# Replacing a build-time list scheduler by stored orders, engine choices and PSUM banks in a four-layer attention kernel

## The chip, the cores and the metric

One core of one Trainium2 chip runs the whole kernel. The metric is the device time of a launch in microseconds; most executions of one kernel agree within 0.3%. A ratio is the mean time of one kernel's fast runs over the mean of the other's from the same rounds on the same chip, so it is not quite the ratio of the medians beside it. 1% of the kernel before is 4.5 us.

PE is the matmul engine, PEld its weight loads, ACT the scalar engine, DVE the vector engine, POOL the general-purpose engine, SP the sync engine, from whose queue all DMAs here start.

## The reference

Four residual layers on x of 2048 rows by 512 features in bfloat16, 32 heads of 16 features; layers A and B alternate, and the second pair reuses the weights of the first:

```python
x = x + A(layernorm(x)); x = x + B(layernorm(x))
x = x + A(layernorm(x)); x = x + B(layernorm(x))
# A, linear attention:
phi = lambda t: where(t > 0, t + 1, exp(t)) + 1e-6
kv = einsum("bhsd,bhse->bhde", phi(k), v);  z = phi(k).sum(s)
o  = (phi(q) @ kv) / (phi(q) @ z + 1e-6)
# B, causal softmax attention over a window of 256 rows:
p = softmax(where(0 <= i - j < 256, q @ k.T * 0.25, -1e9));  o = p @ v
# both end with o.reshape(B, S, D) @ wo
```

A needs a sum over all rows before its first output, so it is a barrier. B's exponentials are most of ACT's work.

## The kernel before

The kernel is not written as loops. It records some 2740 operations in a graph, each with its engine (or two allowed engines), an estimated cost, a priority key, what it reads and writes, and its PSUM tiles. Then, while the program is built, a list scheduler plays the graph against its costs and decides three things: the order on each engine, the engine of each copy that ACT and DVE can both do, and the PSUM bank of each tile (1011 of them reuse one of eight banks).

```python
def pick_banks(banks, held, need):
    if "S" in need:                                   # scores: aligned pairs of banks
        pairs = [b for b in (0, 2, 4, 6) if b in banks and b + 1 in banks]
        n = need["S"] // 2
        return [x for b in pairs[:n] for x in (b, b + 1)] if len(pairs) >= n else None
    free = sorted(banks, key=lambda b: (held[b ^ 1] is None, held[b ^ 1] == "S", -b))
    ...
def schedule(g, par):
    ...
    while done < len(ops):
        t = heapq.heappop(events)                     # simulated time
        ...
        for e in engines:                             # free engine: the ready operation with the lowest key
            if free_at[e] > t: continue
            while ready[e]:
                k, i = heapq.heappop(ready[e])
                ...                                   # skip it if no bank is free
            o.eng, o.t0 = e, start
            got = pick_banks(banks, held, need) if need else []
            ...
            o.deps.extend(u for u in banks.pop(b)[1] if u not in o.deps)
```

The last line: a tile's first matmul waits for the last reader of the tile that had the bank before. A second pass (unchanged) turns all dependencies into semaphore waits; each engine's instruction stream is its list, in the order of the list.

The other piece touched is the transpose of a normalised tile, on PE with a copy out of PSUM, or by a DMA; and the first layer's use of it:

```python
    def transpose(self, name, src, out, rd, wr, key, by_pe):
        if not by_pe:
            return self.on("SP", name, lambda e: e.dma_start_transpose(out(), src()), key, (1310, ...), rd=rd, wr=wr)
        ps = Tile(1, K.cls)
        ...                                           # four 128x128 transposes, then a copy on ACT or DVE
    def layer_a_keys(self, ph, base):
        for t in range(T):
            self.norm(t, ..., [("XQ", t)], True)      # True: transposes of the first stage on PE
            self.a_k(t, k); self.a_v(t, k + 0.05); self.a_q(t, ...)
```

The softmax here doesn't subtract the row's maximum and nothing guards it: scores larger than these inputs give would overflow.

Of the kernel before, what the change touches and what calls it, by code (L numbers as in the profile page):

```python
# [8 lines left out]
ALU = mybir.AluOpType  # L9
# [13 lines left out]
    same=0.0, lat_t=4300, cap_s=8, cap_d=2, cap_e=6, mode=100, sem=35, ring_x=3, wait_s=200,  # L23
# [63 lines left out]
def pick_banks(banks, held, need):  # L87

    if "S" in need:
        pairs = [b for b in (0, 2, 4, 6) if b in banks and b + 1 in banks]  # L90
        n = need["S"] // 2
        return [x for b in pairs[:n] for x in (b, b + 1)] if len(pairs) >= n else None
    free = sorted(banks, key=lambda b: (held[b ^ 1] is None, held[b ^ 1] == "S", -b))
    n = sum(need.values())
    return free[:n] if len(free) >= n else None


def schedule(g, par):

    ops = g.ops  # L100
    for o in ops:
        o.outs, o.nout, o.rdy, o.t0 = [], len(o.deps), 0.0, None
        o.soft = []
        for t in o.tiles:
            t.banks, t.left = None, len(t.users)

    for o in ops:
        for t in o.tiles:
            if t.soft and t.users[0] is o:
                o.soft.extend({d for u in t.users[1:] for d in u.deps if d.i < o.i} - set(o.deps))  # L110
        o.nout += len(o.soft)
        for d in o.soft:
            d.outs.append(o)
    for o in ops:
        for d in o.deps:
            d.outs.append(o)
    engines = ("PE", "ACT", "DVE", "POOL", "SP")
    free_at = dict.fromkeys(engines, 0.0)
    ready = {e: [] for e in engines}
    last_mode = [None, None]  # L120
    banks = {b: (0.0, []) for b in range(8)}
    used = {"S": 0, "D": 0, "E": 0, "K": 0}
    held = [None] * 8
    cap = {"S": par["cap_s"], "D": par["cap_d"], "E": par["cap_e"], "K": 2}
    pending = []
    events = [0.0]
    done = 0

    def release(o):
        if o.nout == 0:  # L130
            heapq.heappush(pending, (o.rdy, o.i))
            heapq.heappush(events, o.rdy)

    for o in ops:
        release(o)
    order = []
    giving = []
    while done < len(ops):
        if not events:
            stuck = [o.name for o in ops if o.t0 is None][:12]  # L140
            raise RuntimeError(f"stuck {stuck} banks {used} {[ (e, [ops[i].name for _, i in ready[e]][:6]) for e in engines]}")
        t = heapq.heappop(events)
        while events and events[0] <= t + 0.5:
            t = max(t, heapq.heappop(events))
        while pending and pending[0][0] <= t:
            _, i = heapq.heappop(pending)
            for e in ops[i].engs:
                k = ops[i].key
                if e == "ACT" and len(ops[i].engs) > 1:
                    k += par["act_bias"]  # L150
                heapq.heappush(ready[e], (k, i))
        while giving and giving[0][0] <= t:
            _, b, cls, users = heapq.heappop(giving)
            banks[b] = (0.0, users)
            held[b] = None
            used[cls] -= 1
        for e in engines:
            if free_at[e] > t:
                continue
            back = []  # L160
            pick = None
            held_back = False
            if e == "PE" and par["same"]:
                ready[e] = [(ops[i].key + (par["same"] if ops[i].mode != last_mode[0] else 0.0), i) for _, i in ready[e]]
                heapq.heapify(ready[e])
            while ready[e]:
                k, i = heapq.heappop(ready[e])
                o = ops[i]
                if o.t0 is not None:
                    continue  # L170
                need = {}
                for x in o.tiles:
                    if x.banks is None:
                        need[x.cls] = need.get(x.cls, 0) + x.n
                if need:
                    if any(used[c] + m > cap[c] for c, m in need.items()) or pick_banks(banks, held, need) is None:
                        back.append((k, i))
                        if "S" in need:
                            n = sum(1 for x in giving if x[0] <= t + par["wait_s"])
                            held_back = held_back or len(banks) + n >= 4  # L180
                        continue
                if held_back and o.end is None and e == "PE" and any(x.banks is None for x in o.tiles):
                    back.append((k, i))
                    continue
                pick = o
                break
            for x in back:
                heapq.heappush(ready[e], x)
            if pick is None:
                continue  # L190
            o = pick
            occ, lat = o.engs[e]
            start = t
            if e == "PE":
                if last_mode[0] is not None and o.mode != last_mode[0]:
                    occ += par["mode"]
                    lat += par["mode"]
                last_mode[0] = o.mode
            o.eng, o.t0 = e, start
            o.end = start + occ  # L200
            o.fin = start + lat + par["sem"]
            need = {}
            for x in o.tiles:
                if x.banks is None:
                    need[x.cls] = need.get(x.cls, 0) + x.n
            got = pick_banks(banks, held, need) if need else []
            for x in o.tiles:
                if x.banks is None:
                    b = got.pop(0)
                    x.banks = [b]  # L210
                    held[b] = x.cls
                    used[x.cls] += x.n
                    o.deps.extend(u for u in banks.pop(b)[1] if u not in o.deps)
                x.left -= 1
                if x.left == 0:
                    for b in x.banks:
                        heapq.heappush(giving, (o.fin, b, x.cls, list(x.users)))
                    heapq.heappush(events, o.fin)
            free_at[e] = o.end
            heapq.heappush(events, o.end)  # L220
            order.append(o)
            done += 1
            for c in o.outs:
                lat_seen = o.end if (e == "PE" and set(c.engs) == {"PE"}) else o.fin
                if o not in c.soft:
                    c.rdy = max(c.rdy, lat_seen)
                c.nout -= 1
                release(c)
    order.sort(key=lambda o: (o.t0, o.i))
    return order  # L230
# [85 lines left out]
class Plan:  # L316
# [33 lines left out]
    def load(self, name, emit, nbytes, wr, key):  # L350
        us = nbytes / 0.2e6 * 1000
        return self.on("SP", name, emit, key, (us, us + 2000), wr=wr)

    def setup(self):
# [13 lines left out]
        for i, (n, f, b, r) in enumerate(seq):  # L368
            self.load(n, f, b, r, key + i)
        i = len(seq)  # L370
        self.load("wBv", lambda e: e.dma_start(K.wBv[:], K.B_wqkv.rearrange("(k p) c -> p k c", p=P)[:, :, 1024:1536]), 524288, [("wBv",)], key + i)
        self.load("wBo", lambda e: e.dma_start(K.wBo[:], K.B_wo.rearrange("(k p) c -> p k c", p=P)), 524288, [("wBo",)], key + i + 1)

        def pool(name, emit, key, ns, **kw):
            return self.on("POOL", name, emit, key, (ns, ns + 60), **kw)
# [43 lines left out]
    def norm(self, t, key, xn_slot, out, wr, by_pe):  # L419
# [4 lines left out]
        self.on("POOL", "eps", lambda e: e.tensor_scalar(K.ve[:, t, :], K.mv[:, t, 1:2], LN_EPS, None, op0=ALU.add), key + 0.02, (190, 260), rd=[("mv", t)], wr=[("ve", t)])  # L424
# [95 lines left out]
    def layer_a_keys(self, ph, base):  # L520
        self.cls = "E"
        for t in range(T):
            k = 100 * ph + t
            self.norm(t, k - 0.5, t % self.par["ring_x"], lambda t=t: self.XQ[:, :, t * P:(t + 1) * P], [("XQ", t)], True)
            self.a_k(t, k)
            self.a_v(t, k + 0.05)
            self.a_q(t, 200 + 4 * (t // 4) + 0.2 * (t % 4) - self.par["k_aq2"])
# [218 lines left out]
    def middle(self, ph):  # L746
# [19 lines left out]
        for i in range(2):  # L766
            self.on("POOL", "zero", lambda e, i=i: e.memset(flat(1536 * i, 1152), 0.0), base - 5, (600, 660), wr=self.room[i])
# [34 lines left out]
class Kernel(Plan):  # L802
# [16 lines left out]
    def run(self):  # L819
# [4 lines left out]
        with ExitStack() as cx:  # L824
# [37 lines left out]
            with nc.Block() as blk:  # L862
                @blk.tensor
                def _(e):
                    play("PE", e)
# [57 lines left out]
```

## Time and profile before

| | before |
|---|---|
| time, median | 453.22 us (453.1 to 453.32) |
| profiled span | 451.5 us |
| busy: PE, DVE, ACT | 89%, 82%, 81% |
| first exponential of the first B layer | 79.9 us |
| from there to that layer's last exponential | 170.4 us |
| from there to the first exponential of the second B layer | 42.1 us |
| from there to its last exponential | 150.7 us |
| tail | 8.4 us |

The five stretches are the stages 1 to 5. They are cut at exponentials because ACT's exponentials mark where each B layer begins and ends whatever the order. Idle time is worth reading only on the engine that leads a stage: PE in 1 and 3, ACT (with PE and DVE close) in 2, ACT in 4. The lines themselves stand in the prediction. Two cautions on the trace of the kernel before: its first exponential starts at 79.75 us, so the cut at 79.9 is 0.15 us late; and it records 7540 matmuls for 7620 weight loads, so 80 matmuls are missing and PE's idle time is read too high.

### The profile page before, as it was taken

How to read it: one execution, taken by the hardware profiler on the slowest of the kernel's cores; microseconds unless marked ns; L12 is line 12 of the kernel's file. 1: busy time of each engine (PE TensorE's matmuls, PEld its weight loads, DVE VectorE, ACT ScalarE, POOL GpSimd, SP SyncE). 2: the span in 40 equal slices, each digit the busy share in tenths (PEclk: the TensorE clock that was granted, in tenths of full speed). 3: DMA queues.
4: the chain of work that ended last, by engine and by line, in shares of the span. 5: the costliest groups of instructions: out<-in, count | busy, mean ns of one | idle time of the engine just before them, and what ended most of it. 6: DMA issues, size and time to landing. Idle time of an engine off the chain costs nothing.

```text
span 451.5 us, 17346 instructions
## 1 busy us (share of the span) xinstructions
PE 400.2 (89%) x7540; PEld 267.7 (59%) x7620; DVE 372.4 (82%) x835; ACT 364.6 (81%) x539; POOL 83.2 (18%) x177
## 2 busy tenths in 40 slices
PE   3899989998998988889999998999899999998765
PEld 1445667666565655556656776766566666665443
DVE  3997798899899989987887839799998999986543
ACT  1555625998999999899999443599999999999982
POOL 7869012012011201120110040210000011000000
PEclk9999999999999999999999999999999999999867
DMA  8800003424433533356422000163344643434321
GB/s 268 290 3 1 1 1 72 109 62 86 97 73 95 89 83 94 70 104 94 73 69 52 15 1 3 49 121 85 91 100 108 102 99 86 111 91 109 68 51 48
DMA packets 63307, 36.39 MB, mean 81 GB/s; under 512 B 43264, under 2 KB 58624, under 8 KB 63232
## 3 DMA queue, kind: packets, MB, share of 16 engines
q1 hardware_dynamic: 63232, 35.28, 34.1%
q8 instruction: 60, 0.98, 1.0%
q14 instruction: 15, 0.12, 0.1%
HBM read 6.29 MB, written 2.10 MB: 19 GB/s over the span
## 4 chain that ended last, share of the span: by engine, by line
ACT 38%; PE 31%; DVE 23%; POOL 4%; issue 3%; POOLq 0%; DVEq 0%
ACT pb L659 28%; PE ps L461 14%; PE ps L475 7%; ACT pb L693 6%; PE ps L718 4%; DVE stats L422 3%; PE ps L645 3%; DVE xres L588 3%; DVE xn L426 2%; DVE pk L486 2%; DVE XQ L486 2%; DVE tE L485 2%; POOL rs L425 2%; ACT pb L660 2%; DVE pb L700 2%
## 5 line engine op out<-in xcount | busy, mean ns | idle before, releaser
L659 ACT ACTIVATE pb<-ps 128x1024 bf16<-128x1024 f32 x224 | 213.3, 1051 | 6.7 <-PE ps L645 6.1
L718 PEld LDWEIGHTS ps<-vB,pb 128*128 128x128 bf16 x2880 | 80.1, 96 | 18.4 <-DVE vA L450 2.7
L718 PE MATMUL ps<-vB,pb 128*128 128x34 bf16 x2880 | 85.8, 178 | 3.4 <-ACT pb L659 0.8
L424 POOL TENSOR_SCALAR ve<-mv 128x1 f32<-128x1 f32 x64 | 17.3, 270 | 299.1 <-DVE mv L423 297.6
L475 PE MATMUL ps<-xT,wBp 128*128 128x128 bf16 x1024 | 67.2, 219 | 2.4 <-DVE o L730 0.7
L666 DVE TENSOR_TENSOR pb<-pb,tri 128x512 bf16<-128x512 bf16 x128 | 53.7, 419 | 18.4 <-ACT pb L659 12.3
L484 ACT ACTIVATE tE<-ps 128x512 bf16<-128x512 f32 x64 | 39.0, 612 | 36.5 <-PE ps L475 18.9
L475 PEld LDWEIGHTS ps<-xT,wBp 128*128 128x128 bf16 x1024 | 58.0, 98 | 11.2 <-issue 3.8
L461 PE MATMUL ps<-wA,XQ 128*128 128x512 bf16 x240 | 61.6, 387 | 2.2 <-DVE o L730 0.4
L645 PE MATMUL ps<-XQ,kB 32*128 32x256 bf16 (+3 forms) x1024 | 50.3, 271 | 13.8 <-ACT pb L659 6.1
L693 ACT ACTIVATE pb<-ps 128x512 bf16<-128x512 f32 x112 | 59.0, 628 | 2.4 <-PE ps L683 2.2
L588 DVE TENSOR_TENSOR xres<-ps,xres 128x512 bf16<-128x512 f32 x64 | 43.8, 685 | 10.1 <-PE ps L461 9.7
L422 DVE BATCH_NORM_STATS2 stats<-xres 128x6 f32<-128x512 bf16 x64 | 43.3, 681 | 4.0 <-DMA xres<-in_A_x_dram 3.6
L645 PEld LDWEIGHTS ps<-XQ,kB 32*128 32x128 bf16 x1024 | 15.3, 93 | 43.8 <-ACT pb L659 23.4
L700 DVE TENSOR_TENSOR pb<-pb,tri 128x1024 bf16<-128x1024 bf16 x56 | 37.4, 674 | 3.9 <-ACT pb L693 3.9
L425 POOL TENSOR_TENSOR rs<-ve,negh 128x1 f32<-128x1 f32 x64 | 38.0, 594 | 5.3
L461 PEld LDWEIGHTS ps<-wA,XQ 128*128 128x128 bf16 x256 | 21.9, 98 | 25.1 <-issue 2.3
L461 PE MATMUL ps<-wBo,oT 128*128 128x512 bf16 x106 | 30.8, 406 | 5.2 <-DVE xn L426 1.4
L475 PE MATMUL ps<-XQ,wA 128*128 128x128 bf16 x512 | 35.3, 219 | 0.1
L426 DVE TENSOR_SCALAR xn<-xres,mv,rs 128x512 bf16<-128x512 bf16 x64 | 28.6, 453 | 6.3 <-POOL rs L425 5.8
L475 PEld LDWEIGHTS ps<-XQ,wA 128*128 128x128 bf16 x512 | 30.2, 98 | 4.7 <-DVE XQ L486 0.6
L461 PE MATMUL ps<-wBv,xT 128*128 128x512 bf16 x110 | 29.6, 380 | 3.3 <-DVE o L730 1.0
(78 smaller groups left out, 463.1 us busy)
## 6 DMA issues: line engine op xcount, KB each, us to landing
vB<-vA SPq DMA_DIRECT2D x128, 68.0 KB, 2.1
kB<-vA SPq DMA_DIRECT2D x64, 128.0 KB, 2.1
out_dram<-xres SPq DMA_DIRECT2D x16, 128.0 KB, 2.0
wA<-in_A_wqkv_dram SPq DMA_DIRECT2D x3, 512.0 KB, 5.9
xres<-in_A_x_dram SPq DMA_DIRECT2D x2, 512.0 KB, 8.5
pb<-in_B_wqkv_dram SPq DMA_DIRECT2D x1, 1024.0 KB, 9.9
xres<-in_A_x_dram SPq DMA_DIRECT2D x3, 256.0 KB, 5.0
wAo<-in_A_wo_dram SPq DMA_DIRECT2D x1, 512.0 KB, 8.6
```

Source lines behind the costliest of these rows:

```text
L422: self.on("DVE", "stats", lambda e: e.bn_stats(K.stats[:, t, :], K.xres[:, t, :]), key, dve(512), rd=[("xres", t)], wr=[("stats", t)])
L425: self.on("POOL", "pow", lambda e: e.tensor_tensor(K.rs[:, t, :], K.ve[:, t, :], K.negh[:], ALU.pow), key + 0.03, (540, 590), rd=[("ve", t ...
L461: m = e.matmul(K.ps(ps), lhs(c), rhs(c), start=c == 0, stop=c == 3)
L475: m = e.matmul(K.ps(ps)[:, f * P:(f + 1) * P], w(c, f), xT(c), start=c == 0, stop=c == 3)
L484: self.on("ACT", "E", lambda e: e.activation(K.tE[:, s, :], K.ps(ps), ACT.Exp, bias=0.0), key, act(512), wr=[("tE", s)], ps=[ps])
L588: self.on("DVE", "res", lambda e: e.tensor_tensor(K.xres[:, t, :], K.ps(po), K.xres[:, t, :], ALU.add), key, dve(512), rd=[("xres", t)], w ...
L645: m = e.matmul(K.ps(ps[gq])[:, 256 * b:256 * b + ns[b]], K.kB[rows, j % 4, 2 * f + b, :, :], K.XQ[rows, f, q:q + ns[b]], start=True, stop= ...
L659: return e.activation(x, bank().rearrange("p g (b n) -> p g b n", b=2), ACT.Exp, bias=0.0, scale=0.25)
L666: return e.tensor_tensor(x, x, K.tri[:, 0, :].unsqueeze(1).unsqueeze(1).to_broadcast([P, 4, 2, 64]), ALU.mult)
L693: return e.activation(K.pb[:, sl, 2 * h:2 * h + 2, :, o:o + 64], i, ACT.Exp, bias=0.0, scale=0.25)
L700: return e.tensor_tensor(x, x, K.tri[:, 1, :].unsqueeze(1).to_broadcast([P, 16, 64]), ALU.mult)
L718: m = e.matmul(K.ps(ps)[:, 34 * u:34 * u + 34], K.pb[:, (b // 2) % 3, gq, f, o:o + P], K.vB[:, (b // 2) % 4, b % 2, r, :], start=i == 0, s ...
```

## The change

Its intent: search for a better schedule off line, starting from critical chains, and store what was found, in place of a scheduler that decides greedily. 338 lines of diff, cut to the core:

```diff
+def place(g):
+    ops = g.ops
+    raw = zlib.decompress(b85decode("".join(TABLE)))
+    n = len(ops)
+    order = [ops[raw[2 * k] + 256 * raw[2 * k + 1]] for k in range(n)]
...
+        o.eng = ("PE", "ACT", "DVE", "POOL", "SP")[raw[2 * n + o.i]]
...
+        x.banks = [raw[3 * n + k]]
...
+            before = held[x.banks[0]]
+            if before:
+                assert all(u.t0 < o.t0 for u in before.users)
+                o.deps.extend(u for u in before.users if u not in o.deps)
-def pick_banks(banks, held, need): ...
-def schedule(g, par): ...
-        order = schedule(self.g, self.par)
+        order = place(self.g)
...
-            self.norm(t, ..., [("XQ", t)], True)
+            self.norm(t, ..., [("XQ", t)], t < self.par["pe_first1"])      # pe_first1=5
-            self.load(n, f, b, r, key + i)
+            self.load(n, f, b, r, key + i if n[0] == "x" or n[:3] in ("wAk", "wAv", "wAq") else 104 + 0.01 * i)
+TABLE = ( ... 60 lines of text ... )
```

Besides the stored schedule: eleven of 16 first-stage transposes go by DMA, weights that are needed late are loaded late, and costs of POOL operations and loads are corrected (which matters only to the search).

## The prediction

> **What bounds the kernel now.** I read first the busy shares and the 40 slices, then a table of engine busy time cut at four moments that I took from the timeline (first exponential of the first sliding-window layer at 79.9 us, its last at 250.3, first of the second such layer at 292.4, last at 443.1), then the chain of waits, and the timeline of the start.
>
> ```profile
> PE 400.2 (89%) x7540; PEld 267.7 (59%) x7620; DVE 372.4 (82%) x835; ACT 364.6 (81%) x539; POOL 83.2 (18%) x177
> ```
>
> Three engines are above 80%: no single bound, and no removal on one engine alone can pay in full. By stage (columns: stretch, its length, busy us of PE, PE weight load, DVE, ACT, POOL, then clock, DMA share, GB/s):
>
> ```profile
> 0.00:79.90 79.90, 66.63 (x713) 41.96 (x725) 64.78 (x145) 38.48 (x67) 40.57 (x85) 1.00 0.30 90
> 79.90:250.30 170.40, 154.72 (x3143) 102.33 (x3169) 150.04 (x344) 161.24 (x236) 21.54 (x50) 1.00 0.41 83
> 250.30:292.40 42.10, 39.61 (x623) 30.30 (x631) 29.75 (x68) 17.08 (x30) 9.58 (x18) 1.00 0.05 14
> 292.40:443.10 150.70, 135.19 (x3046) 91.31 (x3072) 125.32 (x276) 147.17 (x206) 11.54 (x24) 0.97 0.42 94
> 443.10:451.50 8.40, 4.01 (x35) 1.76 (x36) 2.49 (x5) 0.60 (x1) 0.00 (x0) 0.67 0.10 33
> ```
>
> The reader is to see that the limits change. Stage 1 (first linear layer) and stage 3 (second one) are PE's: 39.6 of 42.1 us in stage 3. Stage 4 is ACT's, 147.2 of 150.7: only 3.5 us are idle there. Stage 2 is held by three engines at once; ACT leads with 161.2 of 170.4, so 9.2 us are idle. Stage 5 is a tail in which nobody works much.
>
> ```profile
> 4.09 1.81 POOL spread L378
> 8.02 1.02 POOL spread L394
> 9.37 0.83 POOL spread L394
> 12.50 0.72 DVE xn L426
> 13.55 0.87 DVE tE L485
> ...
> 326.04 7.60 ACT pb L659 x8
> 333.63 1.96 ACT pb L693 x4
> 335.61 7.60 ACT pb L659 x8
> ```
>
> These are the chain that ended last (start, us, what). At the start it runs through constants that POOL builds ahead of the first normalisation. In stage 4 it is a metronome of eight exponentials at 0.95 us and four at 0.49, 9.56 us per block of 128 rows: an order cannot shorten that. The first PE work:
>
> ```profile
> 7.75 1.24 PE L438 MATMUL ps<-ident,xn 128*128 128x128 bf16 x8 [7.75 <-DVE xn L426]
> 9.05 3.57 PE L461 MATMUL ps<-wA,XQ 128*128 128x512 bf16 x8
> 13.61 1.90 PE L461 MATMUL ps<-wA,XQ 128*128 128x512 bf16 x8
> ```
>
> PE starts at 7.75 us, and its first eight wide matmuls take 3.57 us where the next eight take 1.90.
>
> **What the Trainium skill says.** (1) Perfetto Trace Analysis, Identifying the Most-Contended Engine: matmul busy share is a poor measure of distance to the roofline, weight-load busy time a better one; and under Optimization Strategy, a kernel with several regimes may gain by interleaving them. The trace agrees: weight loads are busy 59% where matmuls show 89%, and the five stages have different leaders. (2) TensorE: Matmul & The Clock Gate, The HAM clock gate: matmuls of the first some 3.4 us run at half clock. The 3.57 against 1.90 us above agrees; starting earlier moves this loss, it doesn't remove it. (3) DMA: Bandwidth & Descriptors, DMA Transpose (X-bar): a plain DMA transpose is issued only from the sync or scalar engine. Here all 73 come from the sync queue, at a median 1.27 us of that queue and 2.5 us to landing. (4) TensorE again, Architectural detail: ACT and DVE are strict FIFO. So an instruction listed too early stops all behind it; what an order is worth is just these waits (waits on ACT in the first 80 us: 8.4 us for the query and 7.8 us for the key matmuls).
>
> **The change part by part.** No arithmetic changes; I counted both programs' orders.
>
> *Transposes.* Eleven of 16 tiles in stage 1 (from the sixth on) go by DMA. PE loses 44 matmuls of 128x128: twelve take 0.67 us in the chain, so a tile 0.22 us, 2.5 us together. Eleven copies out of PSUM go too: at 0.49 us of ACT or about 0.34 of DVE (estimate from their 597 and 412 ns less the overlap). Added: eleven sync-queue issues, 11 x 1.27 = 14 us, between about 12 and 50 us where that queue and the DMA are empty (2 to 5 GB/s in slices 3 to 6). They lie beside other work, if they come early enough; the order lists the first eight in a row, right behind the 1 MB weight load.
>
> *PE lists.* Ahead of the first score matmul: minus 2.5 us of transposes, plus 16 query matmuls of 0.056 us (64 take 3.57 us), 0.9: net minus 1.6 us. Between the last score of one layer and the first of the next: minus eight half-products of two wide matmuls each (four value, two output, two windowed-value projections) at 0.445 us (four take 0.89), 3.6 us; minus one group of 24 value matmuls, 0.6; plus two query halves, 0.9, and one denominator group, 0.39: net minus 2.9 us. That work isn't gone: it is listed inside the window layers beside ACT's work (there PE is busy 154.7 of 170.4 us, and 135.2 of 150.7).
>
> *Engine choice.* Copies that either engine can do: in stage 2 ACT has 30 other operations beside the exponentials in place of 35, 5 x 0.48 = 2.4 us less. In stage 4 it has four in place of six, 1 us less. DVE takes them at 0.60 each; over the whole kernel ACT loses 14 operations and DVE gains three.
>
> *Start.* The order puts the first epsilon operation behind seven small POOL constants (0.2+1.8+0.2+0.2+0.3+0.1+0.2 = 3.0 us) instead of eleven plus the big memset, which the trace shows ending at 5.9 us. From 0.8 us that is about 4.1 us, just when the first statistics are done (3.0 + 0.65 + 0.2). Then PE starts near 6 us, not 7.75: minus 1.8 us. Other weights load later; 4.5 MB now stand ahead of the first DMA transpose, at 308 GB/s 15 us, which five tiles of PE work (5 x about 2.8 us) just cover.
>
> *Banks and order.* This is the part without a count. What it can win is the idle time that waits leave. Stage 1: from 9.05 to 79.9 us PE has 60.6 us of listed work (by spacing, e.g. 0.23 us per wide matmul), so some 10 us are lost, 1.7 of it cold clock; I give the search 2 us. Stage 2: 9.2 us idle on ACT; I give it a quarter, 2.5 us. Stage 4: 3.5 idle; 0.7.
>
> *Sum.* Stage 1: 1.8 + 1.6 + 2.0 = 5.4, so 74.5 us. Stage 2: 2.4 + 2.5 = 4.9, so 165.5. Stage 3: 2.9, so 39.2. Stage 4: 1.0 + 0.7, so 149.0. Tail 8.4 unchanged: the chain last exponential, values, division, transpose, output projection, residual, store is the same. Together 436.6 us of span, 14.9 less; the time is 1.7 us above the span before, so 438.3 us, minus 3.3%.
>
> **The rivals.** (a) *The orders give little.* ACT's list in stages 2 and 4 still holds all 400 exponentials, and a list order on paper may be out of step with the chip: a strict FIFO then waits. For it: three engines are near full, so what one wait frees another takes. Against it: the lists are really shorter where the stage's leader is (ACT minus 2.4, PE minus 1.6 and 2.9). Only those 6.9 us plus 1 us in stage 4 would remain: 445 us. (b) *DVE becomes the bound of stage 2.* It takes five copies, 3.0 us, on top of 150.0 of 170.4 busy. At 165.5 us it would be 92% busy; this would halve the stage's gain: 441 us. (c) *DMA transposes come late.* Each lands 2.5 us after issue and they share the rings with 3.5 to 4.5 MB of loads. If the sixth tile came at 22 instead of 18 us, PE would idle some 4 us unless other tiles' work fills it: 441 to 442 us. (d) *The search worked better than I think*: all of ACT's idle time in stage 2 and 5 us of stage 1's go: 6.7 + 3 us more, 429 us.
>
> **Range and chances.** Centre 438.3. (b) and (c) give the upper side, both with part of (a) 446; (d) the lower, 430. The 2% line is 444.2: only (a), or (b) with (c), lies above. I give 0.86 to faster by over 2%, 0.13 to the same, 0.01 to slower, since nothing is added on an engine that leads.
>
> **What would show it right or wrong.** PE's first matmul near 6 us; first exponential near 74.5; ACT's idle time between first and last exponential of the first such layer down from 9 to about 6.5 us; 39 us between the layers with PE over 94% busy; the second such layer 149 us at 9.56 us a block; a tail of 8.4. It is wrong if PE shows long waits for the DMA-written XQ between 15 and 30 us, if ACT waits for scores as often as before, or if the granted clock, now 0.97 in stage 4, falls in more places, because PE then idles in longer pieces.

## The result, and the profile after

The changed kernel takes 434.0 us median (432.52 to 434.44, 4 runs), the kernel before 453.22: ratio 0.957, 95% interval 0.9546 to 0.9595. The forecast was 438.3, in a range of 430 to 446.

Busy shares of the kernel after, then its table by stage (columns as in the prediction):

```profile
PE 402.1 (93%) x7576; PEld 265.4 (61%) x7576; DVE 374.7 (87%) x838; ACT 355.3 (82%) x525; POOL 83.3 (19%) x177
```

```profile
0.00:73.46 73.46, 63.39 (x682) 41.20 (x683) 62.42 (x140) 32.72 (x59) 39.91 (x83) 1.00 0.44 117
73.46:239.39 165.93, 160.79 (x3219) 102.51 (x3218) 154.19 (x353) 160.03 (x231) 22.22 (x52) 1.00 0.42 85
239.39:276.75 37.36, 37.09 (x600) 29.41 (x599) 30.17 (x67) 16.52 (x31) 9.51 (x18) 1.00 0.06 20
276.75:425.22 148.47, 137.28 (x3025) 90.37 (x3024) 124.53 (x273) 145.99 (x204) 11.69 (x25) 0.97 0.41 95
425.22:432.70 7.48, 3.52 (x61) 1.95 (x58) 3.41 (x8) 0.00 (x0) 0.00 (x0) 0.92 0.12 38
```

The arithmetic is the same (PE busy 402.1 us against 400.2 with 80 matmuls unrecorded, DVE 374.7 against 372.4; ACT 355.3 against 364.6, since it has 14 copies fewer); about half of what went is time in which a stage's leader waited. Read the leader of each stage. In stage 2 ACT idled 170.4 - 161.2 = 9.2 us and now 165.9 - 160.0 = 5.9; PE idles 5.1 us there where it idled 15.7 by its trace and 10.7 in e6. In stage 3 PE idled 2.5 us (2.1 in e6, with every matmul recorded) and now 0.3: it is busy 99%. In stage 4 ACT's idle time went from 3.5 to 2.5 us. Stage 3 of e6:

```profile
250.01:292.16 42.15, 40.06 (x630) 30.32 (x631) 29.80 (x68) 17.08 (x31) 9.58 (x18) 1.00 0.05 15
```

Stage 1 needs a second cut, at 15 us, before and after:

```profile
0.00:15.00 15.00, 6.73 (x31) 3.02 (x32) 7.70 (x18) 3.67 (x5) 11.83 (x32) 1.00 0.91 289
15.00:79.90 64.90, 59.90 (x684) 38.94 (x694) 57.07 (x128) 34.81 (x62) 28.73 (x54) 1.00 0.15 44
```

```profile
0.00:15.00 15.00, 5.97 (x28) 3.10 (x28) 9.65 (x24) 4.24 (x7) 11.19 (x30) 1.00 0.87 273
15.00:73.46 58.46, 57.42 (x654) 38.10 (x655) 52.77 (x118) 28.49 (x53) 28.73 (x54) 1.00 0.33 77
```

The first 15 us got no better: PE was busy 6.7 us and is now busy 6.0. Past them PE idled 5.0 us and now 1.0, and its work fell by 2.5 us, as the eleven transposes left. That is the stage's 6.4 us. (Ten of the missing matmuls lie here, 684 against 694 loads. With each filled in behind its weight load at the mean length of its kind, an estimate, the idle time before is about 4.5 us, and the two parts are 3.4 and 2.9 us.) The start after, on PE:

```profile
5.90 0.61 PE L328 MATMUL ps<-ident,xn 128*128 128x128 bf16 x4 [5.90 <-DVE xn L316]
9.31 1.86 PE L351 MATMUL ps<-wA,XQ 128*128 128x512 bf16 x4 [2.81 <-DMA wA<-in_A_wqkv_dram]
```

PE does start at 5.90 us, not 7.75. But the first wide matmul comes at 9.31 us, where it came at 9.05 before: it now waits for the key weights, which are loaded fifth instead of fourth.

Part of the chain that ended last, after, at the end of stage 3 and in stage 4:

```profile
264.42 3.13 PE ps L365 x56
268.63 2.23 PE ps L365 x40
271.09 1.34 PE ps L365 x24
273.15 3.22 PE ps L365 x56
...
288.18 2.06 ACT pb L583 x4
290.26 7.44 ACT pb L549 x8
297.70 1.96 ACT pb L583 x4
```

In stage 3 the chain is now long runs of PE without a break; in stage 4 it is the same metronome as before, 7.44 to 7.57 instead of 7.60 us for eight wide exponentials.

### The profile page after: what moved, and what is told of

Its sections match the earlier page's. It is cut to its first block, busy times and chain, and to the rows that moved or that the text cites. A ratio compares the mean times of both kernels' runs of the same rounds, so it can differ in the third digit from the quotient of the medians.

```text
span 432.7 us, 17332 instructions
## 1 busy us (share of the span) xinstructions
PE 402.1 (93%) x7576; PEld 265.4 (61%) x7576; DVE 374.7 (87%) x838; ACT 355.3 (82%) x525; POOL 83.3 (19%) x177
## 4 chain that ended last, share of the span: by engine, by line
PE 43%; ACT 41%; DVE 9%; DMA 3%; issue 1%; POOL 1%; SPq 1%; POOLq 0%
ACT pb L549 31%; PE ps L351 19%; PE ps L365 10%; ACT pb L583 7%; PE ps L608 6%; PE ps L535 3%; DMA xres<-in_A_x_dram 2%; ACT pb L550 2%; PE ps L402 1%; DVE stats L312 1%; ACT tE L374 1%; DVE xres L478 1%; DMA xT<-xn 1%; DVE xn L316 1%; PE ps L573 1%
## 5 line engine op out<-in xcount | busy, mean ns | idle before, releaser
L549 ACT ACTIVATE pb<-ps 128x1024 bf16<-128x1024 f32 x224 | 211.1, 1050 | 3.7 <-PE ps L535 2.7
L608 PE MATMUL ps<-vB,pb 128*128 128x34 bf16 x2880 | 86.8, 178 | 2.0 <-ACT pb L549 1.0
L351 PE MATMUL ps<-wA,XQ 128*128 128x512 bf16 x256 | 65.9, 387 | 3.2 <-DMA wA<-in_A_wqkv_dram 2.8
L374 ACT ACTIVATE tE<-ps 128x512 bf16<-128x512 f32 x64 | 38.1, 605 | 35.6 <-PE ps L351 16.9
L583 ACT ACTIVATE pb<-ps 128x512 bf16<-128x512 f32 x112 | 60.8, 642 | 1.6 <-PE ps L573 1.2
L556 DVE TENSOR_TENSOR pb<-pb,tri 128x512 bf16<-128x512 bf16 x128 | 52.2, 415 | 8.6 <-ACT pb L550 4.3
L535 PE MATMUL ps<-XQ,kB 32*128 32x256 bf16 (+3 forms) x1024 | 49.9, 270 | 8.4 <-ACT pb L550 2.6
L535 PEld LDWEIGHTS ps<-XQ,kB 32*128 32x128 bf16 x1024 | 15.3, 92 | 37.7 <-ACT pb L549 17.9
L351 PE MATMUL ps<-wBo,oT 128*128 128x512 bf16 x128 | 35.2, 388 | 1.3 <-DVE oT L335 0.5
L351 PE MATMUL ps<-M,pqd 128*128 128x512 bf16 x128 | 34.6, 380 | 0.5 <-DVE pqd L472 0.5
L351 PE MATMUL ps<-wBv,xT 128*128 128x512 bf16 x128 | 33.9, 381 | 0.7 <-DVE vA L495 0.4
```

Of the source, the lines that this page charges most:

```text
L351: m = e.matmul(K.ps(ps), lhs(c), rhs(c), start=c == 0, stop=c == 3)
L374: self.on("ACT", "E", lambda e: e.activation(K.tE[:, s, :], K.ps(ps), ACT.Exp, bias=0.0), key, act(512), wr=[("tE", s)], ps=[ps])
L535: m = e.matmul(K.ps(ps[gq])[:, 256 * b:256 * b + ns[b]], K.kB[rows, j % 4, 2 * f + b, :, :], K.XQ[rows, f, q:q + ns[b]], start=True, stop= ...
L549: return e.activation(x, bank().rearrange("p g (b n) -> p g b n", b=2), ACT.Exp, bias=0.0, scale=0.25)
L556: return e.tensor_tensor(x, x, K.tri[:, 0, :].unsqueeze(1).unsqueeze(1).to_broadcast([P, 4, 2, 64]), ALU.mult)
L583: return e.activation(K.pb[:, sl, 2 * h:2 * h + 2, :, o:o + 64], i, ACT.Exp, bias=0.0, scale=0.25)
```

## The experiments

A schedule is a joint thing, so each part was taken away or done alone with all else frozen. For that the order, engines and banks of either kernel were written into a table for the same `place` function. The kernel before played from such a table was not timed by itself; e6 below, which is that with eleven transposes changed, lands on its time. The experiments were timed in other rounds than the changed kernel, so I compare their ratios to the kernel before, which ran in every round.

My theory after the result: the orders won most, by removing waits; transposes are worth their 2.5 us of PE time; engine choices a little over 3 us. The rivals: the transposes and loads won it; or the banks; or the engines.

| run | what it is | median us | ratio to before (95%) | stages 1 to 5, us |
|---|---|---|---|---|
| after | | 434.0 | 0.957 (0.9546 to 0.9595) | 73.5, 165.9, 37.4, 148.5, 7.5 |
| e1 | new graph, old scheduler | 461.75 | 1.0204 (1.0179 to 1.0229) | 77.4, 169.0, 45.4, 159.4, 7.7 |
| e5 | before, transposes by DMA, rescheduled | 462.41 | 1.0228 (1.019 to 1.0265) | 82.9, 171.8, 40.7, 158.5, 9.6 |
| e6 | before, transposes by DMA, frozen | 453.76 | 0.9997 (0.9969 to 1.0025) | 79.5, 170.5, 42.2, 151.6, 8.9 |
| e7 | after, transposes back on PE | 436.96 | 0.9636 (0.9603 to 0.9669) | 75.9, 166.6, 37.4, 150.0, 7.3 |
| e3 | after, old engine choices | 440.57 | 0.973 (0.9712 to 0.9749) | 73.7, 169.3, 39.5, 148.7, 7.6 |
| e4 | before, new engine choices | 458.49 | 1.0112 (1.0072 to 1.0151) | 81.7, 173.9, 42.7, 151.8, 8.9 |
| e2 low | after, banks: lowest free | 525.22 | 1.1605 (1.1582 to 1.1627) | 79.8, 200.7, 42.9, 191.6, 7.6 |
| e2 pair | after, banks: oldest free | 447.14 | 0.9854 (0.9823 to 0.9884) | 78.1, 169.0, 39.8, 150.7, 7.8 |
| e9 | after, oldest rule for score banks only | 439.01 | 0.9679 (0.9634 to 0.9725) | 72.5, 168.4, 37.4, 151.2, 7.6 |
| e8 | after, first loads in the old order | 435.07 | 0.9583 (0.9561 to 0.9606) | 74.1, 165.8, 37.4, 148.9, 7.5 |
| e10 | after, all loads ahead of transposes | 434.8 | 0.9584 (0.9558 to 0.9611) | 73.4, 166.0, 37.4, 148.7, 7.5 |
| e11 | after's order, oldest banks, old engines | 453.01 | 0.9973 (0.994 to 1.0005) | 79.5, 172.2, 41.1, 151.0, 7.6 |

The stages come from each run's one profiled execution, so they carry its own spread: e9 runs stage 1 with hardly any change and shows 0.9 us less, and the profiled executions of e4, e5 and e7 were 2.5, 2.8 and 1.9 us slower than the medians beside them. All runs gave correct results.

**e1, the new graph under the old scheduler, and e5, one condition changed under it.**

```diff
# e1: the changed kernel
-        order = place(self.g)
+        order = schedule(self.g, self.par)     # and the two functions put back
# e5: the kernel before
-            self.norm(t, ..., [("XQ", t)], True)
+            self.norm(t, ..., [("XQ", t)], t < 5)
```

> The changed kernel's operations (DMA transposes from the sixth tile on, later weight loads, the new costs) but ordered, given engines and banks by the old list scheduler at build time. Theory (the searched orders win most; the other parts are worth the 2.5 us of PE transposes and little else): about 449 us, 446 to 453, and stage 2 still idles ACT some 9 us. Rival (the graph's own changes, transposes and loads and better costs, won it): 434 to 439 us.

> The kernel before with one condition changed: eleven first-stage transposes by DMA, still list scheduled, loads in the old order. Theory: worth at most the 2.5 us of PE time, so 450.5 us, or nothing if they wait behind the 4 MB of loads: 449 to 456. Rival (the transposes are the stage-1 gain of 6 us): 446 to 448.

Both got slower than the kernel before by 2%, outside what either theory or rival said. The stages tell why these two are poor experiments on the transposes: 8 to 9 us of the loss lie in stage 4 (159.4 and 158.5 against 150.7), 200 us after the last first-stage transpose. The list scheduler's keys were tuned for one set of costs; a small edit at the start makes it decide differently to the end. Undoing one part through a scheduler undoes many. What e1 does show: under the old scheduler and its keys the new graph wins nothing; the gain sits in the stored schedule. How much the orders of e1 and e5 differ in stage 4, and which decision did the harm, I did not settle.

**e6 and e7, the transposes with all else frozen.** e6 plays the kernel before from a table in which eleven PE transposes become DMAs at the same place and their copies vanish. e7 puts them back into the changed kernel:

```diff
# e7, in the table: at the place of each of the eleven DMA transposes, or a little behind it
-  T  (SP)
+  T  (PE, four 128x128)   Te (ACT or DVE, copy)   in a PSUM bank that is free there
```

> The kernel before's order, banks and engines, frozen, with only the eleven transposes moved from PE to the DMA queue at the places where they stood; nothing else is rescheduled, unlike the run that let the list scheduler loose and got 462 us. Theory (transposes are worth at most their 2.5 us, less what their 2.5 us to landing costs where nothing was listed between): 450 to 456. Rival (DMA transposes are harmful as such in the first stage, 3 us in the run of 462): 456 or more. Rival (they win stage 1): 447.

> The changed kernel with the eleven transposes put back on PE with their copies, each at or just behind the place of its DMA, in a PSUM bank that is free there; all else frozen. Theory (2.5 us of PE time in a stage that PE leads, and 11 copies on ACT and DVE): plus 2.5 to 5 us, 436.5 to 439. Rival (the order was built round them and each blocks PE until its copy): 442 or more. Rival (off the path): 434.

In the old order the transposes are worth nothing (0.9997). In the new one putting them back costs 0.66% or 3.0 us, of which stage 1 shows 2.4 us. Both are within what the theory expected. Stage 1 past 15 us, e6 and then e7:

```profile
15.00:79.48 64.48, 57.90 (x639) 36.28 (x637) 56.15 (x123) 31.13 (x55) 28.69 (x54) 1.00 0.32 77
15.00:75.86 60.86, 60.06 (x697) 39.99 (x695) 51.80 (x120) 31.88 (x59) 28.11 (x53) 1.00 0.17 52
```

In e6 PE has 2.0 us less work than in the kernel before and idles 1.6 us more; in e7 it has 2.6 us more work than in the changed kernel and idles as little (0.8 against 1.0 us). So the same 2.5 us of PE time pays where PE has no other wait, and goes into waiting where it has.

**e3 and e4, the engine choices.** e3 is the changed kernel with the old scheduler's engine for every copy that has a choice, e4 the kernel before, frozen, with the new ones, except that the copies behind the transposes of normalised tiles stay (34 copies change engine, against 39 in e3).

```diff
# e3: copies by name, changed kernel -> e3
-  V copies of A:  20 ACT, 12 DVE       M copies: 8 ACT
+  V copies of A:  27 ACT,  5 DVE       M copies: 4 ACT, 4 DVE     (net counts; 39 copies change engine in all)
```

> The changed kernel's order and banks, but every copy that either ACT or DVE can do goes back to the engine that the old scheduler chose. Theory (ACT leads in both windowed layers and gets some five copies of 0.48 us back in stage 2, two in stage 4): 437 to 439 us. Rival (engine choice is noise): 433 to 435. Rival (it is the core of the gain): 444 or more.

> The kernel before's order and banks, frozen, with the changed kernel's engine for each copy. Theory (an engine choice is worth something only with the order it was searched with; putting the old ones back into the new order cost 6 us): 452 to 460 us, no gain. Rival (fewer copies on ACT pay anywhere): 447 to 450.

e3 costs 1.6% or 7.2 us, more than the 3.4 us that I had counted from ACT's list and, at 440.57 us, between the theory and the rival that made it the core. Its table by stage, of e3, for stages 2 and 3:

```profile
73.74:243.06 169.32, 161.62 (x3219) 102.71 (x3218) 150.82 (x349) 162.57 (x237) 23.00 (x52) 1.00 0.41 83
243.06:282.56 39.50, 37.81 (x601) 29.34 (x600) 30.73 (x68) 16.16 (x31) 9.67 (x18) 1.00 0.06 19
```

ACT is busy 2.5 us more in stage 2 and idles 6.8 us instead of 5.9: together the 3.4 us that the stage grew. In stage 3, where PE leads, its idle time goes from 0.3 to 1.7 us though no PE operation moved; that PE there waits for copies that come later on the other engine is my reading, not measured apart. e4 shows the other side: the new choices in the old order cost 1.1%, in all five stages a little. An engine choice has no worth of its own; it fits an order or it doesn't.

**e2, the banks.** Order and engines of the changed kernel, banks by two rules, each subject to what is free at that place of the order:

```python
low  = lambda c, last, held, free, is_pair: c[0]                      # lowest free bank or pair
pair = lambda c, last, held, free, is_pair: (                         # last reader listed longest ago,
    min(c, key=last) if is_pair else min(c, key=lambda b: (free(b ^ 1), last(b))))   # halves of broken pairs first
```

> The changed kernel's order and engines, but PSUM banks by a dull rule: the lowest free bank or pair. 609 instead of 299 of the 1000 reused tiles then start within one PE operation of the last read of their bank. Theory (banks are part of what was searched, PE waits for copies when a bank comes back too soon): 442 us, 438 to 448. Rival (the order alone sets the time): 433 to 436.

> The changed kernel's order and engines, banks by a rule that needs no search: the free bank whose last reader is listed longest ago, halves of broken pairs first. 314 of 1000 tiles come within one PE operation of that reader (299 in the changed kernel, 609 in the lowest-bank run that took 525 us). Theory (what matters is how soon a bank is needed again after its last read): 434 to 437 us. Rival (the exact banks matter beyond that distance): 440 or more.

The lowest bank costs 21% on the changed kernel: 525 us. The waits of that run say what happens (engine, line, what it waited for, us in total, times, longest):

```profile
PEld ps L535 <- ACT pb L549: 67.0, 70, 1.7
ACT pb L549 <- PE ps L535: 55.5, 101, 1.7
PE ps L535 <- ACT pb L549: 46.0, 67, 1.6
```

and the same lines of the changed kernel, of which the other two are too small for its list:

```profile
PEld ps L535 <- ACT pb L549: 17.9, 40, 0.9
```

Scores (L535) go into the bank that the last exponentials (L549) have just read: PE waits for ACT, then ACT for PE. All exponentials are still there, but they overlap less with the matmuls: ACT idles 35.7 us in stage 2 and 40.4 in stage 4 where it idled 5.9 and 2.5, and the two stages grow by 35 and 43 us.

The sensible rule was expected to cost nothing or 3 us and cost 2.8%, 12.9 us: here my theory fell. By the share of tiles that come within one PE operation of the last reader its banks are as good as the searched ones (314 against 299). That count is too coarse. Tiles with no PE operation at all in between, counted from the two stored tables, are 85 against 63, and in stage 1, before any scores, 17 against 4 of 68: the rule takes a bank whose partner is held before an older one of a free pair, although no scores need the pair there. Stage 1 of the run, on PE:

```profile
17.67 2.76 PE L351 MATMUL ps<-wA,XQ 128*128 128x512 bf16 x12 [0.85 <-DVE pk L376]
20.27 1.06 PE L365 MATMUL ps<-XQ,wA 128*128 128x128 bf16 x16
21.67 1.04 PE L351 MATMUL ps<-wA,XQ 128*128 128x512 bf16 x4 [0.34 <-ACT vA L340]
...
30.04 0.61 PE L351 MATMUL ps<-wA,XQ 128*128 128x512 bf16 x2 [0.69 <-ACT vA L340]
```

and the changed kernel, same stretch:

```profile
15.06 6.24 PE L351 MATMUL ps<-wA,XQ 128*128 128x512 bf16 x28 [0.39 <-DVE pk L376]
21.14 1.06 PE L365 MATMUL ps<-XQ,wA 128*128 128x128 bf16 x16
22.03 1.03 PE L351 MATMUL ps<-wA,XQ 128*128 128x512 bf16 x4
```

Twenty-eight wide matmuls ran without a break; now they are cut by waits of 0.3 to 0.9 us for a copy on ACT or DVE that has nothing to do with their inputs except the bank. PE's idle time up to the first exponential grows from 10.1 us of 73.5 to 13.1 of 78.1; the rest of the 4.6 us that the stage grows stands in the table as busy time. My reading is that a broken run shows the end of its last matmul each time (28 in a row take 6.24 us, 0.22 each, two alone 0.61). Whether the loss comes from the tiles with nothing in between, or also from when a listed reader really runs, no run separates.

**e9, which banks?** The oldest-pair rule for the score tiles only:

> The changed kernel with only the score tiles' bank pairs chosen by the oldest-pair rule (432 of 624 banks differ, the same mean distance in PE operations, 2.66 against 2.68); all other tiles keep their searched banks. The full rule cost 13 us. Theory (pairs are alike and all are read by ACT in list order, so oldest first is as good; the loss came from the other tiles, whose banks then wait for ACT or DVE readers): 434 to 436 us. Rival (score pairs are where the search paid): 440 to 447.

Plus 1.1%, 4.9 us, in stages 2 and 4 (2.5 and 2.7 us more). That is between the two forecasts: score pairs are not all alike; they hold some 40% of the full rule's loss and the other tiles, by difference, the rest. By stage the two runs fit this: the full rule loses 5.3 us in stages 2 and 4, e9 loses 5.2 there, and 7.0 us of the full rule's loss lie in stages 1 and 3, where e9 changes hardly a bank. The reverse run, other tiles by rule and scores kept, was not made, as the rule found no free bank at one place. The old scheduler's own `pick_banks` was not tried on the new order either.

**e8 and e10, the loads.** The stage-1 profile showed 2.81 us of PE waiting for key weights, so e8 puts the first loads back in the old order; e10 puts the three other late weight loads ahead of the first DMA transpose.

```diff
# order on the sync queue, changed kernel -> e8
-  x0 x1 x2 x4 wAk x6 x8 x12 wAv wAq wBn ...
+  x0 x1 x2 wAk x4 wAv x6 wAq x8 x12 wBn ...
# -> e10
-  ... wAq wBn T T T T T T T T wBv T T wAo T wBo
+  ... wAq wBn wBv wAo wBo T T T T T T T T T T T
```

> The changed kernel with its first ten loads in the old order (key weights third, value weights sixth, the last eight tiles of x after all three weights); all else frozen. In the changed kernel PE's first wide matmul waited 2.81 us for the key weights until 9.31 us. Theory (fixed orders fit their loads; key weights come some 0.8 us sooner, but the statistics of tiles 8 to 15 stand early in DVE's FIFO and now wait for x): 433 to 437 us. Rival (this is left-over waste): 431 to 432.5.

> The changed kernel with the three other late weight loads (1.5 MB) moved ahead of the first DMA transpose, as the kernel before had them; all else frozen. Theory (1.5 MB at some 350 GB/s is 4 us more of full DMA ahead of the transposes, and PE runs out of tiles before the sixth): 436 to 439 us. Rival (transposes are waited for by nobody): 434.

Neither can be told from the changed kernel (intervals overlap). In e8 PE's first wide matmul comes at 7.89 us instead of 9.31, and the next transposes then wait for normalised rows:

```profile
7.89 1.87 PE L351 MATMUL ps<-wA,XQ 128*128 128x512 bf16 x4 [1.39 <-DMA wA<-in_A_wqkv_dram]
10.29 0.60 PE L328 MATMUL ps<-ident,xn 128*128 128x128 bf16 x4 [0.53 <-DVE xn L316]
12.07 1.03 PE L328 MATMUL ps<-ident,xn 128*128 128x128 bf16 x8 [1.18 <-DVE xn L316]
```

So here what came sooner made something else come later; that the start is held by the loads as a whole is my reading. In e10 a matmul does wait for a DMA transpose,

```profile
23.26 0.60 PE L351 MATMUL ps<-wA,XQ 128*128 128x512 bf16 x2 [0.89 <-DMA XQ<-xn]
```

but the stage still ends at 73.4 us. The theory (436 to 439) was wrong and the rival right: putting the late loads late was not part of the gain.

**e11, the order by itself.** The old engine choices and the plain bank rule at once, on the new order:

> The changed kernel's order (and DMA transposes and loads) with the old scheduler's engine choices and the oldest-pair bank rule at once. Apart they cost 1.6% and 2.8% of the kernel before, together 4.4%, just the whole gain. Theory (the three were searched as one and their losses add, so the order by itself is worth about nothing): ratio 0.99 to 1.01, 449 to 458 us. Rival (the losses overlap, since the same waits count in both, and the order keeps a gain of its own): ratio 0.985 or less, 446 us or less. Rival (they multiply): over 1.02.

0.9973, no different from the kernel before (the interval reaches 1.0005), and the stages fall back to those of before (79.5, 172.2, 41.1, 151.0 and 7.6 against 79.9, 170.4, 42.1, 150.7 and 8.4). The two losses add, within the noise: 1.6 and 2.8% apart, 4.0% together. With these banks and engines, which were not searched with it, the searched order keeps nothing that can be told from zero (at most 0.6%), although it still has the DMA transposes and PE's shorter lists.

No experiment gave a kernel that beats the changed one.

## Why the prediction was right

The time (434.0 against 438.3) and the sign were right, and all five stages came within 1.8 us of their forecast. The mechanism is what the tables show: shorter lists on the leader of a stage, and fewer waits on it. But the shares were off. The forecast had 5.2 us of waits in a gain of 14.9; they came to some 9.5 of 18.8, and the gain on PE's start did not come. That the stages fit so well is partly luck, as errors cancelled in stages 1 and 2. Point by point:

- **Start, 1.8 us: wrong.** The step held that PE starting near 6 us would carry through. PE did start at 5.90 us, but I had not followed the key weights, whose load moved from fourth to fifth place. The first wide matmul came 0.26 us later than before. In e8 the weights came 1.4 us sooner, at the price of later rows of x, and nothing was gained.
- **Transposes, 2.5 us: right** in the new order (3.0 us by e7, and 2.5 to 2.9 us less PE work after 15 us). Rival (c), transposes that come late, did not happen: nothing waited for XQ from a DMA, and with 1.5 MB more ahead of them (e10) one matmul waited 0.89 us.
- **Waits of stage 1, 2.0 us: too small.** PE's idle time past 15 us fell by 4.0 us (some 3.4 with the missing records). With the start's missing 1.8 the stage came out at 73.5 instead of 74.5 us: two errors that nearly cancel.
- **Copies taken off ACT in stage 2, 2.4 us: half.** ACT's busy time fell by 1.2 us, and its idle time by 3.3 rather than 2.5 us; sum 4.5 against 4.9. As an effect of its own the term was undersized: undoing all choices costs 7.2 us (e3), not the 3.4 that I counted in stages 2 and 4, as 2.1 us of it lie in stage 3, where I gave engines nothing.
- **Stage 3, 2.9 us: too small, 4.7.** PE's work fell by 2.9 us as counted (40.06 in e6, 37.09 after; 2.5 by the trace that misses records); but PE's 2.1 us of idle time, which I left as it was, fell to 0.3.
- **Stage 4, 1.7 us: right** (2.2). ACT was busy 1.2 us less (two copies fewer, and the exponentials by themselves 0.5 us less) and waited 1.0 us less. The metronome stayed, at 9.4 to 9.6 us a block against 9.57.
- **Tail, unchanged: nearly** (7.5 instead of 8.4 us; why is open).
- **Banks and order, 5.2 us in all, "the part without a count": the step that was sized too low.** By the leaders' idle times the waits fell by 4.0 + 3.3 + 2.2 + 1.0 = 10.5 us in stages 1 to 4, or, with the missing matmuls allowed for, by 3.4 + 3.3 + 1.8 + 1.0 = 9.5. And I treated banks as a detail of the order: they decide 2.8% against a plain rule and 21% against a bad one. Rival (a), that only the shorter lists would remain (445 us), did not happen. Nor do PE's shorter lists pay by themselves: e11 keeps them, with other banks and engines, and is at 453 us.
- **Rival (b), DVE as the bound of stage 2:** DVE is busy 154.2 of 165.9 us, 93%, as forecast, and PE 97%. I saw no sign that DVE took the lead, but no run tests it.
- **Two loose readings, without effect on the sum:** DMA is not empty from 12 us on but moves 366 GB/s from 15 to 20 us, and slices 3 to 6 show 1 to 3 GB/s; and the 8.4 and 7.8 us that ACT waited are those of the window from 20 to 79.9 us, not of the first 80.

## What to carry to other kernels

When three engines are near full and each plays a fixed list, the schedule is one object: the order, the engine of each copy and the PSUM bank of each tile are worth little apart (here 0.3% for the order with plain banks and the old engines, not clear of zero) and 4.3% together, so search them together and store the result. A bank is a wait on its last reader: leave work between that read and the next write. The rule that left none for 352 of 1000 tiles cost 21%; the one with 85, against 63 in the searched banks, cost 2.8%, though how much of that comes from those tiles is not shown. And to learn what one part of a schedule is worth, freeze all else; letting a tuned list scheduler decide again changed stage 4 by 8 us for an edit in stage 1.

## What the Trainium skill lacked or had wrong

- PSUM — Partial Sum Buffer: it states banks, collisions and accumulation rules, but not what the assignment of banks is worth. With order and engines equal it made 434.0, 447.14 or 525.22 us.
- Perfetto Trace Analysis, Matmuls: "Independent matmul groups should rotate through different PSUM banks" is right (rotation against the lowest free bank: 447 against 525 us), but it doesn't say that the choice within a rotation counts: the stored assignment was a further 2.8% faster.
- DMA: Bandwidth & Descriptors, DMA Transpose (X-bar): it gives bandwidths and, for other shapes, a sequencer's cycles, but no time to landing for one transpose between on-chip buffers as issued here. For 128 x 512 bfloat16 the trace has a median 1.26 us of the sync queue and 2.5 us to landing, 4.4 us at most.
